# Gated recurrence and squared-relu layers: two pieces of group 0's second layer in three passes, four of group 1's, and other times for weight parts and attention

## The chip, the cores and the metric

The kernel runs on one core of one Trainium2 chip. The metric is the device time of one execution in microseconds (us); lower is better. A core has TensorE (PE; its weight loads are listed apart as PEld), VectorE (DVE), ScalarE (ACT), GpSimd (POOL), and SyncE (SP), whose queue here issues every DMA. Matrix products are written to PSUM[...].

## What is computed

The reference first runs a gated recurrence over 4 batches, 8 heads, 768 steps, head size 48, and then two layers on its output:

```python
for t in range(S):
    state = alpha[:, :, t, :, None] * state + np.einsum('bhd,bhe->bhde', k[:, :, t], v[:, :, t])
    y[:, :, t] = np.einsum('bhd,bhde->bhe', q[:, :, t], state)
...
x = np.ascontiguousarray(attn_out.transpose(0, 2, 1, 3)).reshape(B * S, H * D)
...
h = np.maximum(x @ w_in, 0.0)
return (h * h @ w_out).astype(np.float32)
```

x has 3072 tokens of 384 numbers; w_in is 384 x 2048, w_out 2048 x 384. The result is wanted in fp32 accuracy.

## The kernel before

**Groups and layers.** The tokens form 24 blocks of 128 (one chunk of steps of one batch, all heads) and six groups of four blocks, 512 tokens each. Per group the kernel runs attention for its blocks, then layer in (x @ w_in, 16 tiles of 128 hidden numbers, each 128x512), squared relu, and layer out (four token blocks, each a sum over 16 hidden tiles, each product 128x384). Both weight matrices are cut in NW = 8 pieces of two hidden tiles. The weights arrive as eight-byte numbers and are rebuilt as fp32 during group 0's layer in.

**Two ways to multiply.** A plain product is one fp32 matmul, which the profile shows as two instructions. The other way is three passes in fp32r: each operand is split into a near part (a of x or h, b of the weight; ACT, L596 and L551), a rest l (DVE, L547) and a difference d (DVE, L600 for x and h, L547 for the weight), and the product is a·b + l·l + d·d with l and d scaled. Group 0's layer in is plain (ffn_in, L805), and so is its layer out (ffn_out, L825). Groups 1 to 5 have layer in in three passes (in_x does a·b and l·l, in_y does d·d, L622). In layer out, out_plain, out_x (a·b, l·l) and out_y (d·d) all go through of_tile (L701). AT['k0'] says how many of the last pieces of group 0's layer out go in three passes, AT['k1'] the same for group 1; groups 2 to 5 have all eight in three passes. Where plain and three-pass pieces are mixed, the plain sum of a token block is copied out on ACT (L723), the sum of a·b and l·l is combined with it on DVE (L737), and the sum of d·d is added on DVE (L547) before the store. Hidden tiles that go in three passes are split by split_h and diff_h, AT['ahead'] tiles before their use.

**Weight parts.** prepare() makes the parts of one piece in four steps, AT['wstep'] apart: cast_w (ACT, L551), rest_w (DVE, L547), scale_w (ACT, L565, and a store of l to DRAM, L556), diff_w (DVE, L547, and a store of d, L556). The near parts b stay on the chip. The l and d parts are loaded again for each later group by pump() (L589) from a list of what comes next, as soon as fewer than room[0] buffers are taken (AT['room1'] in group 1, AT['room'] later); used() gives a buffer back after its last product and calls pump(). The parts of w_in are made first: those named by AT['w_first'] in group 0, the others in group 1 every AT['w_in_by']. The parts of w_out follow: AT['o0'] in group 0, AT['o1'] and AT['o2'] in group 1. The pieces that go in three passes first come first in the list. AT['str1'] is when group 1 puts the d parts of its own pieces on the list.

**Attention.** Blocks go in pairs. ln takes log alpha (ACT, L244), cs its running sum along the chunk (a matmul with a triangle of ones), eb and ei its exponentials. For blocks before SPLIT = AT['split'], cs is one fp32 matmul (L265); for the others DVE first splits log alpha into hi and lo (L256, L257), and cs is two fp32r matmuls (L268, L269). turn transposes q and k (L482). ga computes scores (L372) and state sums (L395) of the pair's first block and most of y of the pair before (L352), gb the rest of y and the second block. next_state (L421) multiplies the state by the last row of decays, which comes back by DMA (last<-row, L303). ev_part copies y into x (L515, mostly ACT). split_x and diff_x split x for layer in of the next group.

**What sets the order.** There is no automatic scheduler: weave() goes through the list of units of the current group (matmul steps, each with a cost, about one per 0.66 us of PE) and, ahead of each unit, calls the events that are due. An event's due time is in units since the group's start, and each call puts its instructions on the engines' queues there and then. So AT's numbers move instructions within the queue of every engine. Attention of the next group, splits of x, weight parts and loads are all events:

```python
            while events and events[0][0] <= at:
                _, e, given = events.pop(0)
                e(*given)
            f(*args)
            at += cost
```

AT['g0'] and AT['g1'] are the starts of the pairs of blocks in groups 0 and 1, AT['g'] those in later groups; 'ga' and 'gb' say how long after a pair's start its ga and gb come, in groups 1 to 5; 'g0x', 'g1x' and 'gx' are when the splits of x start; 'h0' and 'h1' where the first splits of h stand among the plain units, 'h1by' how far apart; 'evs0' the distance of the copies of x in group 0. All PSUM tiles come from one pool of eight banks, taken in turn.

Of the kernel before, what the change touches and what calls it, by code (L numbers as in the profile page):

```python
# [15 lines left out]


GB = 4
AT = {'evs': 0.4, 'lead': 4, 'post': 3, 'w_first': (43, 45, 47, 49), 'wstep': 1.6, 'w_in_at': 2, 'w_in_by': 3, 'room1': 23, 'room': 25, 's0': 4, 'ahead': 5, 'late': 2, 'xs': 0.2, 'g0': (-0.5, 19.5, 27.5), 'sc0': (2.35, 2.35, 2.35), 'g1': (0.5, 17.0, 30.5), 'g': (2.2, 15.0), 'g1x': 51, 'gx': 47, 'g0x': 54.5, 'k0': 0, 'h0': 16, 'k1': 5, 'h1': 4, 'h1by': 4, 'evs0': 0.3, 'tp': 'ADMD', 'tp1': 'ADAD', 'split': 12, 'o0': (52,), 'o1': (16, 24), 'o2': (20, 26, 30, 37, 38), 'str1': 25.5, 'ga': 9, 'gb': 12.5}


RUN = {0: 128, 32: 32, 64: 64, 96: 32}
# [3 lines left out]
def kernel(  # L26
# [220 lines left out]

    SPLIT = AT["split"]

# [318 lines left out]
    def diff_w(w, p):  # L568
# [5 lines left out]
        for x in "ld":  # L574
            t = made.pop((x, w, p))
            if w == "i" or p >= NW - AT["k0"] or (x == "l" and p >= NW - AT["k1"]):
                here[x, w, p] = t
        pump()

    def prepare(at, w, p):  # L580
        step = AT["wstep"]
        fs = (cast_w, rest_w, scale_w, diff_w)
        return [(at + i * step, f, (w, p)) for i, f in enumerate(fs)]
# [78 lines left out]
    def splits_of_x(at, g):  # L662
        return [(at + i * AT["xs"], f, (g, i % KM)) for i, f in enumerate((split_x,) * KM + (diff_x,) * KM)]

    def layer_in(g):
        units = []
        for n in range(NJ + 2):
            if n < NJ:
                units.append((1.05, in_x, (n,)))
            if 0 <= n - 2 < NJ:  # L670
                units.append((0.53, in_y, (n - 2,)))
            if 0 <= n - AT["post"] < NJ:
                units.append((0, in_post, (n - AT["post"],)))
            if AT["lead"] <= n < AT["lead"] + AHEAD and (g > 1 or AT["k1"] == NW):
# [355 lines left out]
```

## Time and profile before

| | us |
|---|---|
| median of three runs | 523.61 |
| lowest, highest | 522.91, 525.53 |
| the profiled execution | 524.45 |
| span of that execution in the profile | 522.7 |
| group 0: until its layer in / its layer in / its layer out | 36.0 / 44.8 / 49.2 |
| group 1: layer in / layer out | 41.3 / 47.2 |
| groups 2, 3, 4, 5 | 80.3, 79.2, 75.0, 69.7 |

The granted clock of TensorE was 1.00 throughout. The stages are cut by the first and last products of each kind on PE. In the profile, a row of the timeline gives the start in us, the length, the engine, the line of the kernel, what is written and what is read, shapes, how many instructions; in square brackets stands how long the engine had been idle and for whom. A piece of the chain of waits gives start, length, and what ran. A matmul's end is modelled, and rows of matmuls overlap, so paces are read from starts.

### The profile page before, as it was taken

What the parts mean: (1) busy time and instruction counts of PE and PEld (TensorE: products, weight loads), DVE (VectorE), ACT (ScalarE), POOL (GpSimd) and SP (SyncE); (2) the same over time, 40 slices, a digit from 0 to 9 for tenths busy, and PEclk for the clock granted to TensorE, in tenths of its full rate; (3) what the DMA queues carried; (4) which work ended last, traced back from release to release, by engine and by line L of the source; (5) the groups of instructions that cost most, each with busy time, mean ns of one, the idle gap of its engine ahead of it and who ended that gap; (6) DMA issues with size and microseconds to landing.
All of it is one profiled execution on the core that took longest, in us unless ns stands there. A gap on an engine that the chain in (4) does not pass through costs nothing.

```text
span 522.7 us, 12883 instructions
## 1 busy us (share of the span) xinstructions
PE 514.0 (98%) x5268; PEld 418.0 (80%) x5268; DVE 355.4 (68%) x611; ACT 312.7 (60%) x648; POOL 5.3 (1%) x29
## 2 busy tenths in 40 slices
PE   8989999999999999999999999999999999999997
PEld 5764455665787679978899988899988899988997
DVE  4698989864576789766587466588465477363861
ACT  4658785676888797375863275953275774064620
POOL 4000000000000000000000000000000000000000
PEclk9999999999999999999999999999999999999999
DMA  9899677244586983998975787874673544898201
GB/s 150 204 255 232 207 233 221 47 137 182 164 201 183 249 208 120 285 336 219 226 218 177 235 250 197 213 201 148 231 258 132 167 138 141 260 347 287 84 0 60
DMA packets 140850, 101.95 MB, mean 195 GB/s; under 512 B 111460, under 2 KB 114552, under 8 KB 140792
## 3 DMA queue, kind: packets, MB, share of 16 engines
q1 hardware_dynamic: 140792, 101.14, 67.3%
q8 instruction: 41, 0.67, 0.5%
q14 instruction: 17, 0.14, 0.1%
HBM read 83.79 MB, written 17.33 MB: 193 GB/s over the span
## 4 chain that ended last, share of the span: by engine, by line
PE 93%; DVE 2%; DMA 2%; SPq 1%; issue 1%; ACT 0%; DVEq 0%
PE o L701 33%; PE h L622 32%; PE o L825 8%; PE h L805 7%; PE y L352 4%; PE T L482 2%; PE sckv L372 2%; PE sckv L395 2%; PE cs L265 2%; DMA qk_lent<-in_q_dram 1%; SPq L303 1%; SPq L109 1%; DMA a_in<-in_alpha_dram 1%; DVE x L515 0%; PE cs L268 0%
## 5 line engine op out<-in xcount | busy, mean ns | idle before, releaser
L622 PE MATMUL h<-xa,wb 128*128 128x512 f32 x240 | 69.6, 398 | 0.0
L622 PE MATMUL h<-xd,wd 128*128 128x512 f32 x240 | 68.5, 398 | 0.1
L622 PE MATMUL h<-xl,wl 128*128 128x512 f32 x240 | 67.7, 390 | 0.0
L547 DVE TENSOR_TENSOR hid<-h,hid 128x512 f32<-128x512 f32 x40 | 27.6, 689 | 55.2 <-PE h L622 51.4
L515 ACT COPY x<-y 32x256 f32<-32x256 f32 (+2 forms) x132 | 47.2, 365 | 24.1 <-PE y L352 18.6
L639 ACT ACTIVATE h<-h 128x512 f32<-128x512 f32 x40 | 23.3, 581 | 61.2 <-PE h L622 61.2
L622 PEld LDWEIGHTS h<-xl,wl 128*128 128x128 f32 x240 | 45.0, 188 | 9.8
L622 PEld LDWEIGHTS h<-xd,wd 128*128 128x128 f32 x240 | 44.2, 188 | 10.2 <-issue 0.5
L701 PE MATMUL o<-wd,hd 128*128 128x384 f32 x296 | 52.1, 334 | 0.0
L622 PEld LDWEIGHTS h<-xa,wb 128*128 128x128 f32 x240 | 44.3, 188 | 9.7
L701 PEld LDWEIGHTS o<-wd,hd 128*128 128x128 f32 x296 | 51.4, 188 | 0.0
L701 PE MATMUL o<-wb,ha 128*128 128x384 f32 x152 | 50.9, 335 | 0.0
L701 PE MATMUL o<-wl,hl 128*128 128x384 f32 x152 | 50.9, 335 | 0.0
L701 PE MATMUL o<-wb,hx 128*128 128x384 f32 x144 | 48.7, 338 | 0.0
L701 PE MATMUL o<-wl,hx 128*128 128x384 f32 x144 | 48.1, 334 | 0.0
L805 PE MATMUL h<-x,w_in 128*128 128x512 f32 (+1 forms) x108 | 43.6, 551 | 1.2 <-ACT x L515 1.2
L825 PE MATMUL o<-w_out,hid 128*128 128x384 f32 x128 | 42.8, 490 | 0.0
L637 ACT ACTIVATE hid<-h 128x512 f32<-128x512 f32 x40 | 23.9, 599 | 27.8 <-PE h L622 27.7
L805 PEld LDWEIGHTS h<-x,w_in 128*128 128x128 f32 x108 | 19.9, 190 | 21.1 <-issue 17.2
L825 PEld LDWEIGHTS o<-w_out,hid 128*128 128x128 f32 x128 | 23.9, 190 | 16.0
L547 DVE TENSOR_TENSOR hl<-hid,ha 128x512 fp32r<-128x512 f32 x38 | 26.1, 687 | 7.5 <-ACT ha L596 7.5
L596 ACT ACTIVATE ha<-hid 128x512 fp32r<-128x512 f32 x38 | 23.7, 633 | 11.4 <-PE o L701 6.1
(117 smaller groups left out, 896.1 us busy)
## 6 DMA issues: line engine op xcount, KB each, us to landing
wd<-do SPq DMA_DIRECT2D x37, 384.0 KB, 3.2
wl<-li SPq DMA_DIRECT2D x32, 384.0 KB, 4.8
wd<-di SPq DMA_DIRECT2D x32, 384.0 KB, 4.5
wl<-lo SPq DMA_DIRECT2D x32, 384.0 KB, 4.2
raw<-in_moe_w_in_dram SPq DMA_DIRECT2D x8, 768.0 KB, 6.6
raw<-in_moe_w_out_dram SPq DMA_DIRECT2D x8, 768.0 KB, 6.7
v_in<-in_v_dram SPq DMA_DIRECT2D x24, 192.0 KB, 5.0
out_dram<-osb SPq DMA_DIRECT2D x24, 192.0 KB, 1.9
```

The source lines that it names most:

```text
L265: nc.tensor.matmul(out=out, lhsT=causal, rhs=blk[n].pop("la"), start=True, stop=True)
L352: ins = nc.tensor.matmul(out=ys[e][64 * half : 64 * half + D + G * e, m % 2, p // 2, t], lhsT=lhsT, rhs=rhs, start=(half, e) not in seen, ...
L372: nc.tensor.matmul(out=ps[e][HALF[h], 0, p, :], lhsT=ks[rows, p, HALF[h]], rhs=qs[rows, p, HALF[h]], start=True, stop=True, skip_group_che ...
L515: copy(out=x[kk][to : to + m, t : t + 2], in_=blk[n]["y"][e][r : r + m, :, p // 2],)
L547: nc.vector.tensor_tensor(out=o, in0=x, in1=z, op=op)
L596: nc.scalar.activation(out=a, in_=x, func=AF.Copy, scale=NEAR)
L622: nc.tensor.matmul(out=acc["h", j], lhsT=here[w, "i", p][:, kk, jj * 128 : (jj + 1) * 128], rhs=x_parts[x][:, kk], start=start and kk == 0 ...
L637: nc.scalar.activation(out=hid[j], in_=x, func=AF.Copy, scale=E)
L639: nc.scalar.activation(out=x, in_=x, func=AF.Copy, scale=1.0 + E)
L701: nc.tensor.matmul(out=acc[t][:, 0:DM], lhsT=lhs[:, t * C : (t + 1) * C], rhs=rhs, start=start, stop=stop, skip_group_check=True,)
L805: nc.tensor.matmul(out=ps, lhsT=w[:, kk, c0 : c0 + 128], rhs=xT[g][kk][:, cols], start=(kk == 0), stop=(kk == KM - 1),)
L825: nc.tensor.matmul(out=acc[t][:, 0:DM], lhsT=hid[per * i + j][:, t * C : (t + 1) * C], rhs=w_out[i][:, j, :], start=(i == 0 and j == 0), s ...
```

## The change

Only the dictionary AT at line 19 changes. In words: k0 goes from 0 to 2 and k1 from 5 to 4. Group 0 prepares three pieces of w_in instead of four, and two of w_out (6 and 7) instead of one (3); group 1 prepares five of w_in and six of w_out, in the order 4, 5, 0, 1, 2, 3. Blocks 10 and 11 take cs in fp32r (split 10). The pairs of blocks in group 1 start later, the third of group 0 half a unit later, and ga comes one unit later in groups 1 to 5. The splits of x come one unit earlier in groups 1 to 5 and one later in group 0; hidden tiles are split six tiles ahead instead of five. room1 is 22 instead of 23 and str1 24 instead of 25.5. Group 0's units come to 58.5 instead of 60.

```diff
-AT = {'evs': 0.4, 'lead': 4, 'post': 3, 'w_first': (43, 45, 47, 49), 'wstep': 1.6, 'w_in_at': 2, 'w_in_by': 3, 'room1': 23, 'room': 25, 's0': 4, 'ahead': 5, 'late': 2, 'xs': 0.2, 'g0': (-0.5, 19.5, 27.5), 'sc0': (2.35, 2.35, 2.35), 'g1': (0.5, 17.0, 30.5), 'g': (2.2, 15.0), 'g1x': 51, 'gx': 47, 'g0x': 54.5, 'k0': 0, 'h0': 16, 'k1': 5, 'h1': 4, 'h1by': 4, 'evs0': 0.3, 'tp': 'ADMD', 'tp1': 'ADAD', 'split': 12, 'o0': (52,), 'o1': (16, 24), 'o2': (20, 26, 30, 37, 38), 'str1': 25.5, 'ga': 9, 'gb': 12.5}
+AT = {'evs': 0.4, 'lead': 4, 'post': 3, 'w_first': (46.0, 49.5, 53.0), 'wstep': 1.6, 'w_in_at': 2, 'w_in_by': 3.4, 'room1': 22, 'room': 25, 's0': 4, 'ahead': 6, 'late': 2, 'xs': 0.2, 'g0': (-0.5, 19.5, 28.0), 'sc0': (2.35, 2.35, 2.35), 'g1': (2.5, 19.5, 35.0), 'g': (2.2, 15.0), 'g1x': 50, 'gx': 46, 'g0x': 55.5, 'k0': 2, 'h0': 18, 'k1': 4, 'h1': 4, 'h1by': 2, 'evs0': 0.8, 'tp': 'ADMD', 'tp1': 'ADAD', 'split': 10, 'o0': (40, 47), 'o1': (), 'o2': (23, 26, 29, 35, 42, 36), 'str1': 24, 'ga': 10, 'gb': 12.5}
```

## The prediction

> **What bounds the kernel now.** I read the page's header first, then the chain of waits in order of time, then timelines of the places that the change touches. In the header PE is busy nearly all of the span, DVE two thirds, ACT three fifths:
>
> ```profile
> span 522.7 us, 12883 instructions
> PE 514.0 (98%) x5268; PEld 418.0 (80%) x5268; DVE 355.4 (68%) x611; ACT 312.7 (60%) x648; POOL 5.3 (1%) x29
> PE 93%; DVE 2%; DMA 2%; SPq 1%; issue 1%; ACT 0%; DVEq 0%
> ```
>
> Read in the last line that the chain runs through PE for 93%; the rest lies almost all in the first 36 us (loads and the first blocks). After that the largest idle stretches on PE are a late third-pass weight part at 222.8 us (about 0.3) and an "issue" gap at 261.6 (0.28), so what counts is how long PE's instructions take. The chain gives their pace without the modelled ends (start, length, piece of chain):
>
> ```profile
> 121.23 9.23 PE o L825 x28
> 175.07 5.36 PE o L701 x16
> 269.46 29.32 PE o L701 x168
> 453.19 32.68 PE h L622 x144
> ```
>
> L825 and the x16 of L701 are fp32 products of layer out, two instructions each: 9.23 / 28 x 2 = 0.659 us per product of 128x384. The x168 are products in three passes: 29.32 / 168 x 3 = 0.524. So a product in three passes is 0.136 cheaper. The other price is that of cs, the running sum of logs (first two rows of group 1's layer in, then group 2's):
>
> ```profile
> 162.91 0.81 PE L265 MATMUL cs<-a_in,causal 128*128 128x384 f32 x2
> 163.26 1.16 PE L622 MATMUL h<-xd,wd 128*128 128x512 f32 x3
> 164.25 0.85 PE L622 MATMUL h<-xa,wb 128*128 128x512 f32 x3
> ...
> 248.65 0.34 PE L268 MATMUL cs<-hi,causal_r 128*128 128x384 f32 x1
> ...
> 249.36 0.63 PE L622 MATMUL h<-xa,wb 128*128 128x512 f32 x2
> ```
>
> From the fp32 cs to the second group of L622 pass 1.34 us. Three L622 matmuls of it are 3 x 0.227 (32.68 / 144) = 0.68, so a cs costs 0.66; part of it shows only as a late start of the matmul after it. In two fp32r passes, two blocks take 249.36 - 248.65 = 0.71, or 0.355 each.
>
> **The skill.** "Perfetto Trace Analysis", Identifying the Most-Contended Engine, says that busy matmul time doesn't measure headroom, since matmuls overlap. The trace agrees: the L701 rows are 334 ns long and start 174.5 ns apart; I price by starts. "TensorE: Matmul & The Clock Gate", Back-to-back issue gap, gives N / 2.4 + 2.5 ns for an isolated warm matmul, 162.5 ns at N = 384; the trace has 174.5, and the trace decides. It has no row for fp32. The same page, Architectural detail, calls ACT and DVE strict FIFOs: an instruction that waits holds everything behind it. The trace agrees: in
>
> ```profile
> 242.72 0.36 DVE L421 TENSOR_TENSOR s<-s,last 128x192 f32<-128x192 f32 x1 [3.82 <-DMA last<-row]
> 243.00 0.68 DVE L651 SCALAR_TENSOR_TENSOR hid<-hid 128x512 f32<-128x512 f32 x1
> 243.60 0.68 DVE L547 TENSOR_TENSOR hid<-h,hid 128x512 f32<-128x512 f32 x1
> ```
>
> DVE stands 3.82 us for a DMA, and the eviction of h behind it ends at 244.28, just before PE goes on at about 244.4.
>
> **The change, part by part.**
> (1) k0 0 to 2: in group 0, pieces 6 and 7 of layer out go to three passes: 4 hid tiles x 4 token blocks = 16 products x 0.136 = -2.17 us of PE.
> (2) k1 5 to 4: in group 1, one piece goes back to fp32: 8 x 0.136 = +1.08.
> (3) split 12 to 10: blocks 10 and 11 take the fp32r cs: 2 x (0.66 - 0.355) = -0.61.
> PE's work: -2.17 + 1.08 - 0.61 = -1.70 us. All of it lies on the path, as PE doesn't wait there.
> (4) Added beside PE: group 0 splits four hid tiles, group 1 two fewer, so two more in all: ACT 2 x 0.63 (L596), DVE 2 x (0.69 + 0.69) (L547, L600). Group 0 also gets 4 combinations at L737 (0.55) and 4 at L547 (0.56), and blocks 10 and 11 need hi and lo, 2 x (0.35 + 0.56). About 9 us of DVE over the run; the cover is DVE's 32% of idle time, except at the seam in (5).
> (5) The seam from group 0 to group 1. Before, the splits of x stand here:
>
> ```profile
> 127.06 1.67 ACT L596 ACTIVATE xa<-x 128x512 fp32r<-128x512 f32 x3
> 127.72 1.90 DVE L547 TENSOR_TENSOR xl<-x,xa 128x512 fp32r<-128x512 f32 x3 [3.55 <-ACT xa L596]
> 129.53 1.89 DVE L600 SCALAR_TENSOR_TENSOR xd<-xa,xl 128x512 fp32r<-128x512 f32 x3
> 130.00 1.15 PE L622 MATMUL h<-xa,wb 128*128 128x512 f32 x3
> 130.99 0.39 PE L622 MATMUL h<-xl,wl 128*128 128x512 f32 x1
> ```
>
> The last xl is ready at 129.6, PE needs it at about 131.4: 1.8 us of slack. I walked the new order by laying its instructions end to end at these paces. PE gets there some 2.2 us sooner, while ACT still has the twelve copies of x (L515, 0.37 each, now placed later), a scaling of a weight part (L565, 0.74) and a cast (L551, 0.74) to do between about 121 and 126.6; only then come the three xa. From 126.7, with ACT at 0.55 per xa and DVE at 0.6 per xl, the last xl ends near 129.1 to 129.3, and PE would want it near 128.9. Stall 0.2 to 0.8; I take 0.4. Zero if ACT is a little faster; 1.5 if the weight part's DVE work (0.95 each for rest and diff) holds up xl too. The new L737 of the first token block ends about when PE wants its sum: nothing to 0.3, within that range.
> (6) Weight parts. Group 0 still prepares five pieces (3 of w_in + 2 of w_out, before 4 + 1), group 1 eleven (5 + 6, before 4 + 7). ACT, DVE and the two stores per piece on SP are the same in number and only move past loads and last<-row on SP's queue. The fourth w_in piece now comes in group 1: by my walk its l is cut by 149.1 and wanted at 152.2, the tightest later one has 1.4 us. Cost 0; without the cover, at most 1.4 each.
> (7) Loads. Group 1 has to load the l parts of pieces 6 and 7 again (two more wl<-lo), one wd<-do fewer. With room1 22, the d parts of 6 and 7 are issued late in group 1, at about 207.3 and 208.5, and wanted at about 214.5 and 214.9: 6.4 to 7.2 us. The loads of L589 in the profile took:
>
> ```profile
> DMA to landing us min/median/max: 3.0/3.9/6.0
> ```
>
> So they land in time, by 0.4 at worst as sampled; I take 0.1, between 0 and 4 (a third-pass d part at 222.8 was late already). "DMA: Bandwidth & Descriptors", Latency and other measured facts, has about 2 us of fixed cost per DMA; here even the quickest part takes 3.0.
> (8) ga 9 to 10, ahead 5 to 6, the pairs of group 1 2 to 4.5 units later, gx and g1x a unit earlier, evs0. These move attention, the splits of h and those of x against PE's stream, with no instruction added (ga's empty instruction on POOL goes along; POOL is 1% busy). ga one unit later meets the wait for last<-row later, which shortens it; ahead 6 gives each split one more tile of lead. I count 0, from -0.5 (the small gaps at 222.8 and 261.6 vanish) to +1.5 (a score bank or an eviction comes later than PE wants it, about 0.3 in each of five groups).
>
> Sum: -1.70 + 0.4 + 0.1 = -1.2 us. The profiled execution took 524.45 with a span of 522.7; it would become 523.25 and 521.5. The median shown is 523.61, 0.84 below the profiled run; from it the forecast is 523.61 - 1.2 = 522.4. Half a per cent, 2.6 us, is about what a measurement of this kernel tells from no change (its three runs spread over 522.91 to 525.53).
>
> **Rivals.**
> A. PE's saving arrives whole and the two small gaps go too: -1.70 - 0.3 - 0.3 = -2.3, so 521.3. For it: PE hardly waits today. Against it: the slack at the seam is less than the 2.2 us by which PE comes sooner.
> B. The seam takes it: the stall is 1.5 or more and a second small one follows (the xd splits, 0.6 each, and the first evictions behind the same queue): -1.70 + 2.0, so 523.9. For it: ACT's queue is full for 5 us there. Against it: my walk has the last xl late by 0.8 at most.
> C. Slower: the d parts of pieces 6 and 7 land late at the end of group 1. The load of 7 stands on SP behind the store of a d part of piece 2, which waits for DVE's difference. If it lands in 10 us instead of under 6.4, PE stands 3.6 us; the loads for group 2 behind it (the next one was late by 0.3 already) add perhaps 1.4: -1.70 + 0.4 + 5.0 = +3.7, so 527.3. It decides from a landing of about 6.4 us. For it: DMA is 78% busy in this stage and the wait is for one queue. Against it: no load of this line took over 6.0.
> That the change doesn't do what it says can be left out: the order of instructions shows 16 products more and 8 fewer in three passes, and two fp32 cs fewer.
>
> **Chances.** The forecast, with its own range 521.6 to 523.3, 0.48; A 0.19; B 0.16; C 0.17. Under 521.0 lies most of A (0.15); over 526.2 nearly all of C (0.16); within half a per cent 0.69. The range of 520.7 to 525.9 takes in A with the bound of -0.5 of (8), the forecast, B, and leaves most of C out.
>
> **What would show it.** The chain should show runs of L701 x16 and x32 instead of L825 in group 0, 0.66 per fp32 product and 0.52 in three passes, as before, with 0.7 for the two cs of blocks 10 and 11. PE's first L622 of group 1 should start at about 128, with a wait of 0.2 to 0.8 for xl; without a wait A is right, with over 1.5 B. PE's row L701 wd,hd at about 214 to 215 without a wait for a DMA refutes C. I am wrong if PE's cadence changes where fp32 and fp32r products alternate, or if waits for h or sckv appear in groups 2 to 4, where no product changes.

## The result, and the profile after

The changed kernel takes 523.0 us (median of 20 runs) against 524.77 for the kernel before, run beside it (20 runs): ratio 0.9973, 95% interval 0.9963 to 0.9982. That is 1.4 us less (0.9 to 1.9), where 1.2 were forecast, and inside the half per cent that had the highest chance. The profiled execution has a span of 521.0 us.

The header of the page after, and its chain by engine:

```profile
span 521.0 us, 12919 instructions
PE 511.3 (98%) x5276; PEld 418.5 (80%) x5276; DVE 364.6 (70%) x627; ACT 312.9 (60%) x650; POOL 5.3 (1%) x29
PE 93%; DVE 2%; SPq 2%; DMA 2%; issue 1%; ACT 0%; DVEq 0%
```

PE still carries 93% of the chain. DVE has 9 us more work, as the sum of part (4) had it, and "issue" comes into view. In the chain in order of time (start, length, piece), the pieces at which the stages begin, and one that nobody forecast:

```profile
35.23 9.72 PE h L805 x26
79.76 9.03 PE o L701 x28
120.31 7.41 PE o L701 x40
127.72 6.41 PE h L622 x27
175.70 1.47 PE y L352 x89
202.00 1.41 PE y L352 x88
203.41 1.07 issue
204.48 0.33 PE y L352 x4
217.87 6.17 PE h L622 x27
267.81 29.32 PE o L701 x168
297.13 6.17 PE h L622 x27
```

The paces are those of before: 29.32 / 168 again. At 203.41 PE stands 1.07 us for nothing that the profile shows, in the middle of the y products (L352) of group 1. The run of y around it takes 2.81 us in all, the one at 175.70 takes 1.47: the gap costs 1.3 to 1.4 us, about 0.3 more than the wait that is listed.

The same pieces in the chain of before:

```profile
36.27 9.72 PE h L805 x26
130.46 4.10 PE h L622 x18
218.53 4.12 PE h L622 x18
298.78 6.17 PE h L622 x27
```

Cutting both chains at the first long run of L805 and at the first L622 of each group gives the account:

| stretch | before | after | difference | forecast |
|---|---|---|---|---|
| until the x26 run of L805 | 36.27 | 35.23 | -1.04 | 0 |
| group 0 from there | 94.19 | 92.49 | -1.70 | -2.17 + 0.4 = -1.77 |
| group 1 | 88.07 | 90.15 | +2.08 | +1.08 - 0.61 + 0.1 = +0.57 |
| group 2 | 80.25 | 79.26 | -0.99 | 0 (-0.5 to +1.5 for all of part 8) |
| groups 3 to 5 | 223.92 | 223.87 | -0.05 | 0 |

The first row is no effect of the change: five other kernels with the same first instructions (the moves alone, split 12, k0 0, k1 4 and ga 9 below) start that run at 35.2 to 35.4, among them k1 4, which is the kernel before but for one number. The one profiled execution of before was about 1 us late there. So the sum of the two profiles agrees with the medians partly by luck, and it is the stages that have to be explained: group 0 as forecast, groups 1 and 2 not.

The seam between groups 0 and 1, from ACT's, DVE's and PE's timelines:

```profile
126.23 1.67 ACT L596 ACTIVATE xa<-x 128x512 fp32r<-128x512 f32 x3
126.89 1.90 DVE L547 TENSOR_TENSOR xl<-x,xa 128x512 fp32r<-128x512 f32 x3 [0.91 <-ACT xa L596]
127.56 0.89 PE L622 MATMUL h<-xa,wb 128*128 128x512 f32 x3
128.29 1.05 PE L622 MATMUL h<-xl,wl 128*128 128x512 f32 x3
129.18 0.86 PE L622 MATMUL h<-xa,wb 128*128 128x512 f32 x3
```

PE begins group 1 at 127.6, as forecast (about 128), while the last xl ends at 128.8. The three products with xl take 129.18 - 128.29 = 0.89 instead of 0.68. The page's groups of weight loads show the same wait, and a smaller one at the new L737:

```profile
L622 PEld LDWEIGHTS h<-xl,wl 128*128 128x128 f32 x240 | 45.1, 188 | 10.0 <-DVE xl L547 0.4
L701 PEld LDWEIGHTS o<-wd,hd 128*128 128x128 f32 x304 | 52.8, 188 | 0.3 <-DVE osb L737 0.3
```

The load is late by 0.4, but PE loses less here: the chain's run of L701 x40 is 7.41 - 40 x 0.1745 = 0.43 over its pace and the x27 of L622 0.24 over the 6.17 of other groups. Some 0.2 of the first is the usual cost of coming back from y, so the seam costs about 0.4 to 0.5.

### The profile page after: what moved, and what is told of

The parts are those of the page before. It is cut to its first block, busy times and chain, and to the rows that moved or that the text cites. A ratio compares the mean times of both kernels' runs of the same rounds, so it can differ in the third digit from the quotient of the medians.

```text
span 521.0 us, 12919 instructions
## 1 busy us (share of the span) xinstructions
PE 511.3 (98%) x5276; PEld 418.5 (80%) x5276; DVE 364.6 (70%) x627; ACT 312.9 (60%) x650; POOL 5.3 (1%) x29
## 4 chain that ended last, share of the span: by engine, by line
PE 93%; DVE 2%; SPq 2%; DMA 2%; issue 1%; ACT 0%; DVEq 0%
PE o L701 41%; PE h L622 32%; PE h L805 7%; PE y L352 4%; PE T L482 2%; PE sckv L372 2%; PE sckv L395 2%; PE cs L265 1%; DMA qk_lent<-in_q_dram 1%; SPq L109 1%; SPq L303 1%; DMA a_in<-in_alpha_dram 1%; PE cs L268 0%; PE cs L269 0%; DVE x L515 0%
## 5 line engine op out<-in xcount | busy, mean ns | idle before, releaser
L622 PE MATMUL h<-xa,wb 128*128 128x512 f32 x240 | 68.2, 393 | 0.0
L622 PE MATMUL h<-xd,wd 128*128 128x512 f32 x240 | 68.0, 399 | 0.0
L622 PE MATMUL h<-xl,wl 128*128 128x512 f32 x240 | 67.9, 391 | 0.0
L701 PE MATMUL o<-wb,ha 128*128 128x384 f32 x160 | 54.7, 342 | 0.0
L701 PE MATMUL o<-w_out,hid 128*128 128x384 f32 x160 | 54.0, 491 | 0.0
L701 PE MATMUL o<-wd,hd 128*128 128x384 f32 x304 | 53.8, 335 | 0.0
L701 PE MATMUL o<-wl,hl 128*128 128x384 f32 x160 | 53.6, 335 | 0.0
L622 PEld LDWEIGHTS h<-xl,wl 128*128 128x128 f32 x240 | 45.1, 188 | 10.0 <-DVE xl L547 0.4
L701 PEld LDWEIGHTS o<-wd,hd 128*128 128x128 f32 x304 | 52.8, 188 | 0.3 <-DVE osb L737 0.3
L622 PEld LDWEIGHTS h<-xa,wb 128*128 128x128 f32 x240 | 44.7, 188 | 9.3 <-ACT xa L596 0.2
L622 PEld LDWEIGHTS h<-xd,wd 128*128 128x128 f32 x240 | 44.2, 188 | 9.6
L701 PE MATMUL o<-wb,hx 128*128 128x384 f32 x144 | 48.7, 338 | 0.0
L701 PE MATMUL o<-wl,hx 128*128 128x384 f32 x144 | 48.2, 335 | 0.0
L701 PEld LDWEIGHTS o<-w_out,hid 128*128 128x128 f32 x160 | 29.9, 190 | 19.3
L805 PE MATMUL h<-x,w_in 128*128 128x512 f32 (+1 forms) x108 | 43.6, 552 | 1.2 <-ACT x L515 1.2
L596 ACT ACTIVATE ha<-hid 128x512 fp32r<-128x512 f32 x40 | 25.6, 640 | 25.1 <-DVE hx L547 15.8
L805 PEld LDWEIGHTS h<-x,w_in 128*128 128x128 f32 x108 | 20.0, 190 | 21.0 <-issue 16.9
L547 DVE TENSOR_TENSOR hl<-hid,ha 128x512 fp32r<-128x512 f32 x40 | 27.5, 688 | 10.0 <-ACT ha L596 10.0
```

The source lines that it names most:

```text
L547: nc.vector.tensor_tensor(out=o, in0=x, in1=z, op=op)
L596: nc.scalar.activation(out=a, in_=x, func=AF.Copy, scale=NEAR)
L622: nc.tensor.matmul(out=acc["h", j], lhsT=here[w, "i", p][:, kk, jj * 128 : (jj + 1) * 128], rhs=x_parts[x][:, kk], start=start and kk == 0 ...
L701: nc.tensor.matmul(out=acc[t][:, 0:DM], lhsT=lhs[:, t * C : (t + 1) * C], rhs=rhs, start=start, stop=stop, skip_group_check=True,)
L805: nc.tensor.matmul(out=ps, lhsT=w[:, kk, c0 : c0 + 128], rhs=xT[g][kk][:, cols], start=(kk == 0), stop=(kk == KM - 1),)
```

## The experiments

"Gaps taken off" below means: span, less the start of the x26 run, less the "issue" waits listed for PE. It is 484.7 for the changed kernel (521.0 - 35.23 - 1.1) and 486.1 for the one before (522.7 - 36.27 - 0.3): with one gap each, the change without start and gaps is worth 1.4 us. As a gap costs about 0.3 more than its listed wait, a kernel with more of them comes out too high by about 0.3 for each.

**The moves alone.**

```diff
-'k0': 2, 'k1': 4, 'split': 10
+'k0': 0, 'k1': 5, 'split': 12
```

> The times of the changed kernel with k0 0, k1 5 and split 12 as before: only the moves. If the gain is PE's work alone, this gives it all back (+1.7 us against the changed kernel) and takes away the wait at the seam (-0.4): within 0.5 us of the kernel before, ratio 0.999 to 1.001. If the moves themselves bring about 1 us (the gaps in group 2 that the profile after no longer shows), the ratio is about 0.998.

Measured: 536.0 us, ratio 1.0203 (1.0182 to 1.0223). Both expectations miss by 10 us. PE's waits in this kernel:

```profile
PE T L482 <- DVE k_in L284: 3.3, 1, 3.3
PE T L482 <- DVE q_in L284: 2.8, 2, 2.3
PE o L701 <- issue: 1.4, 1, 1.4
PE y L352 <- issue: 1.2, 1, 1.2
```

Group 1 takes 230.12 - 129.47 = 100.65 us, 10.5 more than in the changed kernel; the chain leaves PE from 184 to 206 and runs through ACT's copies of x and the splits of weights and of ten hidden tiles on DVE, one after the other. With k1 5 and the new times they fall together; k1 4 leaves eight tiles to split. Split 12 alone and k0 0 alone (below) bring nothing of this size, which points to k1 5, though the changed kernel with k1 5 alone was not run. The new times are no gain in themselves.

**Split 12.**

```diff
-'split': 10
+'split': 12
```

> The changed kernel with split 12. By PE's prices the two cs of blocks 10 and 11 cost 0.66 instead of 0.355 each again: +0.6 us against the changed kernel, ratio to before about 0.9985; in the profile two fp32 cs with 1.34 us to the second L622 group after each. If DVE's hi and lo of these blocks held something up, the ratio stays at 0.997 or falls.

Measured: 523.79 us, ratio 0.9975 (0.9962 to 0.9988). The timing can't tell 0.6 us, but the profile can: gaps taken off, 521.6 - 35.17 - 1.2 = 485.2, +0.5 against the changed kernel, and the two fp32 cs are back:

```profile
161.74 0.81 PE L265 MATMUL cs<-a_in,causal 128*128 128x384 f32 x2
162.09 1.15 PE L622 MATMUL h<-xd,wd 128*128 128x512 f32 x3
163.08 0.81 PE L265 MATMUL cs<-a_in,causal 128*128 128x384 f32 x2
```

From one cs to the next 1.34 us, with three L622 in between: the price of 0.66 per cs stands.

**Group 0 in fp32.**

```diff
-'k0': 2
+'k0': 0
```

> The changed kernel with k0 0: group 0's layer out all fp32. Theory of PE's prices: 16 products x 0.136 = +2.2 us, less the wait at the seam of about 0.4, so +1.8 against the changed kernel, ratio to before about 1.0007. Rival, that the seam took more than 0.5: +1.2 or less, ratio under 0.9997.

Measured: 526.93 us, ratio 1.0029 (1.0015 to 1.0043): 3 us over the changed kernel, not 1.8. Group 0 takes 129.58 - 35.39 = 94.19, +1.70 against 92.49, about the 1.8 expected; its first L622 x27 takes 6.14, so the wait at the seam is gone. The rest is "issue" again, now at three places and 3.0 us instead of 1.1:

```profile
PE y L352 <- issue: 1.6, 2, 1.1
PE o L701 <- issue: 1.4, 1, 1.4
```

Gaps taken off it is 486.7, +2.0; with 0.3 more for each of three gaps against one, it is about +1.4, a little under the 1.8 expected.

**One piece fewer in group 1, in the kernel before.**

```diff
-'k1': 5
+'k1': 4
```

> The kernel before with k1 4 alone: one piece of group 1's layer out in fp32. By PE's prices 8 products x 0.136 = +1.1 us in group 1, ratio 1.002, plus or minus what the gaps at the ends of instruction blocks do, as PE's stream is 16 instructions shorter from there (up to 1 us). Rival, that PE waited for parts of the fifth piece: no loss or a gain.

Measured: 525.85 us, ratio 1.0026 (1.001 to 1.0042). Group 1 takes 218.46 - 129.37 = 89.09 against 88.07 before: +1.02, for 1.08 worked out. Group 2 has two gaps of "issue", 1.1 in all, where before had 0.3.

**What the gaps are.** They stood at different places in different kernels. I counted PE's instructions in each trace in order of start (matmuls, weight loads, and semaphore instructions, from 0) up to each gap within a stretch of work. The last instruction ahead of the gap was number 4544 in the changed kernel and with split 12, 6080 in the kernel before, 3776 and 4544 with the moves alone, 3776, 5312 and 6080 with k0 0, 5312 and 6080 with k1 4. All are 192 past a multiple of 256; the waits for DVE stand anywhere. The page lists what brings instructions in:

```profile
q8 instruction: 42, 0.69, 0.5%
```

0.69 MB in 42 packets for 10,704 PE instructions: about 16.4 KB and 256 instructions per packet (the Trainium skill, "Perfetto Trace Analysis", The 4-stage abstract model, has them at 64 bytes each, which agrees). And the 256 instructions ahead of a gap mostly went by in 1.9 to 2.0 us, in the runs of scores, state sums and y (ga), against 521 / 42 = 12 us on average. So I took the gap for PE running out of instructions, and moved the ends of the blocks by putting instructions ahead of everything:

```diff
-    for _ in range(3):
+    for _ in range(2):
         warm(0)
+    ps = ps_att.tile([128, NP, 64], FP32, tag="att", name="small")
+    for _ in range(17):
+        nc.tensor.matmul(
+            out=ps[0:64, 0, :], lhsT=s_t[0][0:D, 0, :], rhs=s_t[0][0:D, 1, :],
+            start=True, stop=True,
+        )
```

> The changed kernel with one warm-up matmul fewer and 17 small ones of zeros at the start, where PE waits for its first inputs: 64 PE instructions more, ahead of everything. Theory: the gap of 1.07 us at 203.4 is PE out of instructions, which arrive in blocks of 256; both gaps seen (203.4 after, 261.3 before) stand 192 instructions past a multiple of 256, each at the end of a block that PE ran through in 1.9 us. With 64 more the block ends elsewhere, no block goes by in under 2.5 us, and the gap is gone: about -1 us against the changed kernel, ratio to before 0.995 to 0.9955. Rival, that the gap is a wait for data at that product: it stays, ratio 0.9973.

Measured: 525.41 us, ratio 1.0013 (1.0004 to 1.0022): slower, where -1 was expected. The products at the start were not free: 34 instructions took 3.82 us, all to one place of PSUM, and the x26 run began at 38.44 instead of 35.23. But the gap at y in group 1 is gone, and one stands at another place and line, again 192 past a multiple of 256 (number 7360):

```profile
322.39 0.96 PE L628 MATMUL h<-xl,wl 128*128 128x512 f32 x3 [0.85 <-issue]
```

A wait for data would have stayed at its product. Gaps taken off it is 484.7, the changed kernel's own number. Then the shift through the filler matmuls of the prologue, by two sizes:

```diff
+    fillers = [7, 7, 7, 7]
...
-        for _ in range(3):
+        for _ in range(fillers.pop(0)):
             nc.tensor.matmul(
-                out=ps[:, 0:NP, :], lhsT=s_t[3].rearrange("a p d -> a (p d)")[:, 0:128],
-                rhs=s_t[3], start=True, stop=True,
+                out=ps[:, 0:2, :], lhsT=s_t[3].rearrange("a p d -> a (p d)")[:, 0:128],
+                rhs=s_t[3][:, 0:2, :], start=True, stop=True,
```

The other size has [12, 12, 11, 11] and 0:1 for 0:2.

> The changed kernel with the 12 filler matmuls of the prologue (4 calls of 3, 256 columns, while PE waits for inputs) as 28 of 128 columns: 64 PE instructions more and no work on the path. Theory of blocks of 256 instructions: the gap of 1.07 at 203.4 is gone; the only gap left is at most the 0.9 seen in group 3 with the same shift. Against the changed kernel -0.2 to -1.1 us, ratio to before 0.995 to 0.997; start of the first L805 run in the chain as before, 35 to 36 us. Rival (a wait for data): gap at the same product of y in group 1.

> The same with 46 fillers of 64 columns: 136 PE instructions more. Here the trace of the changed kernel has five blocks of 256 instructions that PE runs through in under 2.8 us (near 99, 316, 339, 394 and one more), against two. Theory: gaps come at the ends of such blocks, at 192 past a multiple of 256, where transfers are busy: 0 to 3 of them, 0.5 to 1.5 us each, so against the changed kernel -1 to +2.5 us, and none at 203.4. Rival (a wait for data): gap at the same product of y in group 1, and no other.

Measured: 522.86 us, ratio 0.9962 (0.9951 to 0.9974), with one gap of 0.4 in group 3 (number 7360 again), none at 203.4; and 527.3 us, 1.0047 (1.0029 to 1.0066), with three gaps:

```profile
PE y L354 <- issue: 1.0, 1, 1.0
PE o L703 <- issue: 1.0, 1, 1.0
PE h L624 <- issue: 0.5, 1, 0.5
```

They are numbers 2240, 5568 and 8128, all 192 past a multiple of 256, and again none at y of group 1. The x26 run starts at 36.95 and 38.94, as the fillers cost time after all. With starts and gaps taken off the two are at 484.75 and 484.9: between the shifts, little else changed. So the gap at 203.4 belongs to PE's instruction stream and not to data.

That PE waits for the next block of instructions can be read from the traces, which hold the start and length of every q8 packet. Each is 16,384 bytes. Taken in order, packet number k fits the block that begins after number 256 k + 192 (times in us; a stop is counted from one start to the next):

| block end | its packet is over | last start before | next start | after the packet |
|---|---|---|---|---|
| changed kernel, 4544 | 203.04 | 203.19 | 204.48 | 1.44 |
| kernel before, 6080 | 260.13 | 261.07 | 261.56 | 1.43 |
| k0 0, 3776 | 179.23 | 178.65 | 180.66 | 1.43 |
| shift with small products, 7360 | 317.14 | 318.06 | 318.48 | 1.34 |
| changed kernel, 3776 (no stop) | 174.94 | 176.66 | 176.66 | 1.72 |

In the fourteen profiles PE passes 528 such ends after the first 40 us. It stops at 21 of them (19 are listed as "issue", two are too short for that), and each time goes on 1.24 to 1.66 us after the packet was over. At the other 507 the packet had been over for 1.39 us or more when PE came, and it doesn't stop. So a gap appears where PE runs through its block before the next packet has been over for about 1.4 us; near 175 the changed kernel runs through a block as fast, but its packet came in time. What delays a packet in one place and not in another was not looked into.

**ga back to 9.**

```diff
-'ga': 10
+'ga': 9
```

> The changed kernel with ga 9 as before. By part (8) of the prediction the later ga is worth nothing by itself: within 0.4 us of the changed kernel once the gaps at the ends of instruction blocks are taken off, ratio to before 0.996 to 0.999 with them. Rival: the later ga is what removed the loss in group 2 (the profile of before lost about 0.9 us there): +0.5 to +1 us with the gaps taken off, in group 2.

Measured: 524.08 us, ratio 0.9984 (0.9972 to 0.9997). Group 2 takes 297.75 - 218.41 = 79.34 against 79.26, so the later ga isn't what removed the loss there. Gaps taken off (1.2) it is 485.15, +0.45. This kernel has two gaps in group 1, so about 0.3 of it is the second gap's cost beyond its listed wait, and the rest is inside the 0.4 expected.

**The seam earlier.**

```diff
-'w_first': (46.0, 49.5, 53.0), 'evs0': 0.8
+'w_first': (45.0, 48.5, 52.0), 'evs0': 0.4
```

> The changed kernel with the copies of x in group 0 closer together (evs0 0.4) and the three w_in pieces of group 0 prepared one unit earlier: ACT gets to the splits of x sooner. If ACT's queue is what makes PE wait at the seam, the last xl comes about 0.7 us sooner and the wait of about 0.4 to 0.5 us goes: -0.3 to -0.5 against the changed kernel, ratio to before about 0.9965. Rival: DVE's combinations (L737) or the weight parts set it, and it stays: 0.997 or above.

Measured: 524.25 us, ratio 0.9986 (0.9975 to 0.9997): it got worse, by 1.1 with gaps taken off. DVE's and PE's timelines:

```profile
122.21 0.69 DVE L547 TENSOR_TENSOR hl<-hid,ha 128x512 fp32r<-128x512 f32 x1 [1.30 <-ACT ha L596]
122.94 0.69 DVE L600 SCALAR_TENSOR_TENSOR hd<-ha,hl 128x512 fp32r<-128x512 f32 x1
123.55 0.95 DVE L547 TENSOR_TENSOR wd<-wb,wl 128x768 fp32r<-128x768 f32 x1
124.42 0.95 DVE L547 TENSOR_TENSOR wl<-w_in,wb 128x768 fp32r<-128x768 f32 x1
125.29 1.95 DVE L737 SCALAR_TENSOR_TENSOR osb<-o,osb 128x384 f32<-128x384 f32 x4
125.89 3.04 PE L701 MATMUL o<-wd,hd 128*128 128x384 f32 x16 [1.19 <-DVE osb L737]
```

With the weight parts earlier, ACT scales and casts them ahead of the split of the last hidden tile; DVE stands 1.30 for that split, then has two weight parts in its queue ahead of L737, and PE waits 1.19 for L737 before out_y. The three xa begin at 127.34 instead of 126.23, so the earlier xl that was expected did not come about. Two settings moved at once, and whether ACT's copies set the wait for xl stays untested. What the run shows is that at the seam things queue on DVE and ACT, and one that moves up pushes another back.

**A third piece in group 0.**

```diff
-'w_first': (46.0, 49.5, 53.0), 'g0': (-0.5, 19.5, 28.0), 'g0x': 55.5, 'k0': 2, 'h0': 18, 'o0': (40, 47), 'o2': (23, 26, 29, 35, 42, 36)
+'w_first': (45.0, 48.5, 52.0), 'g0': (-0.5, 19.5, 27.2), 'g0x': 54.7, 'k0': 3, 'h0': 14, 'o0': (36.5, 41, 46), 'o2': (26, 29, 35, 42, 36)
```

> The changed kernel with a third piece of group 0's layer out in three passes (k0 3), with its parts prepared in group 0 and the splits and copies placed to suit. By PE's prices 8 products x 0.136 = -1.1 us against the changed kernel, and ratio to before 0.995, if ACT and DVE still cover it. Rival: ACT and DVE are full in that stage (L596, L547, L600 for six hidden tiles and three pieces of weight parts), the wait at the seam grows from about 0.4 to 1.5 or more, and nothing is gained: 0.997 or above.

Measured: 525.16 us, ratio 1.0002 (0.9989 to 1.0015). The rival was right:

```profile
PE o L701 <- DVE osb L737: 2.3, 1, 2.3
```

Here ACT and DVE no longer hide behind layer out of group 0; two pieces are about what they cover as these events are placed.

**The shift without its cost, and with the earlier seam.** In the last filler call one filler instead of three, and 18 small products to different places of PSUM:

```diff
+    more = [0, 0, 0, 18]
...
-        for _ in range(3):
+        for _ in range(1 if more[0] else 3):
...
+        for i in range(more.pop(0)):
+            half = 64 * (i % 2)
+            nc.tensor.matmul(
+                out=ps[half : half + 64, i // 2 % 8, :], lhsT=s_t[3][0:D, 0, :],
+                rhs=s_t[3][0:D, 1, :], start=True, stop=True, skip_group_check=True,
+            )
```

> The shift by 64 PE instructions again, now without a cost in the prologue: two fillers fewer in the last filler call, 18 small products to different places of PSUM instead. As with the first try of this shift, no gap at 203.4, at most 0.6 to 0.9 in group 3, and the first L805 run of the chain at 35 to 36 us instead of 37. Against the changed kernel -0.3 to -1.0 us: ratio to before 0.9955 to 0.9965.

> Both of the last two together, the candidate to beat both kernels: sum of the two, -0.6 to -1.4 us against the changed kernel, ratio to before 0.9948 to 0.9962.

Measured: 522.03 us, ratio 0.994 (0.9922 to 0.9958), and 523.64 us, 0.9977 (0.9961 to 0.9993). The first is faster than both kernels: its interval lies below the changed kernel's 0.9963 to 0.9982 (each taken against the kernel before, in separate sessions). It is a little better than expected. The x26 run starts at 35.32, and group 1 takes 216.56 - 127.77 = 88.79 instead of 90.15: without its gap it is 1.36 shorter. PE's list of waits has no "issue" in it, but group 3 has a stop of 0.4 from start to start at number 7360, too short for that list. The second has the seam's 1.2 at L737 again and a gap of 0.7 at number 7360, so the sum expected of it did not come about.

## Why the prediction was right, point by point

- (1) k0: -2.17 with a wait of 0.4. Group 0 became 1.70 shorter, and undoing k0 alone gave 1.70 back. The mechanism was right, the price 8% too high. The run of 9.23 from which 0.659 was read follows products of y, and coming back from them costs about 0.2; a run x28 that follows cs takes 9.03 (79.76 in the chain after), which gives 9.03 / 28 x 2 = 0.645. From start to start the median is 322 to 323 ns for an fp32 instruction of layer out and 173 in three passes, before and after: 0.126 per product. That makes k0 -2.02, k1 +1.01 and PE's sum -1.62.
- (2) k1: +1.08. Alone in the kernel before, +1.02 in group 1. Right, and nearer still to 1.01.
- (3) split: -0.61. Undone alone, +0.5 once the gaps are off. Right within what one profile tells.
- (4) DVE's 9 us: 364.6 - 355.4 = 9.2. No wait outside the seam shows them, as said. The third piece in group 0 shows how little cover is left: PE waits 2.3 us.
- (5) The seam: 0.4 forecast, about 0.5 found, half in group 0 and 0.24 in group 1's first L622 run, at xl and a little at L737. The size was about right. The order that was walked on ACT is the one in the trace (copies, scaling, cast, then xa); no run shows what the wait would be without it.
- (6) Weight parts at no cost: no wait on them in the profile after. But the moves alone show that the new times cost 11 us, gaps included, where k1 is 5.
- (7) The late d parts: PE's chain has no wait at 212 to 218. The loads of L589 took

```profile
DMA to landing us min/median/max: 3.0/3.9/6.7
```

 The d parts of pieces 6 and 7 were issued at 204.3 and 205.7, about 3 us earlier than worked out. The second landed 6.0 us later, at 211.7, and its products begin at about 215. So rival C did not come, with 3 us to spare instead of 0.4 at worst: the issue times, not the landing, were off.
- (8) Moves at 0, down to -0.5: group 2 lost 0.99. In before it has

```profile
222.78 2.32 PE h L622 x9
260.20 1.09 PE y L352 x67
261.29 0.28 issue
261.56 0.57 PE y L352 x22
```

 The first 27 L622 took 225.10 - 218.53 = 6.57 instead of 6.17, because of the late d part at 222.8, and the run of y 1.94 instead of 1.41. So the two cost 0.40 and 0.53, nearly all of the 0.99. Both are gone, which rival A had as -0.6. The gap of before was the end of an instruction block; the 0.40 also went with k1 4 alone and is absent with ga 9, so it is not the later ga that removed it.
- Missed: the new gap in group 1, which costs 1.36. Its like had been visible before, as the 0.28 at 261.6, which I took for a small fixed loss. Without it, group 1 is 0.72 over before (88.79 - 88.07), for 0.57 forecast: that is +1.08 - 0.61 and the 0.24 of the seam, and nothing for late loads.

So the terms of PE's sum were right one by one, within 8%. The total came out near -1.2 partly by luck: what it left out, -0.99 in group 2 and +1.36 in group 1, largely cancels. How long start and gaps were in the executions that were not profiled isn't known; the 20 runs of before spread over 522.9 to 527.3 us, those of the changed kernel over 522.7 to 524.9. The kernel with the shift and no cost at the start is 0.6% faster than the kernel before, but that compares it with a before whose own gap was not moved away; with gaps and start off both, the change is worth the 1.4 us above, of which 0.40 is the late d part of before.

## What to carry to other kernels

Where one engine is busy all the time, price a change by the start-to-start pace of its instructions, stage by stage, and compare stages of two traces, not only spans: start-up and gaps of 1 us can hide or feign an effect of this size. When every queue is nearly full, an event that is moved up pushes another back, so the times of a plan belong to the amounts that they were made for. And look at the place of a wait that nothing explains: here it stood at a fixed count of instructions.

## What was unexpected of the hardware

PE can stand in the midst of ready work at the end of a block of 256 of its instructions. In the fourteen profiles all 19 "issue" gaps of PE over 0.15 us after the first 40 us (0.3 to 1.4 us) stood at the same count within the block, after blocks that went by in 1.9 to 3.3 us, and PE went on about 1.4 us after the packet with the next block was over. Small fp32 products of 48x64 that all wrote one place of PSUM took 0.11 us per instruction (3.82 / 34); those to different places took about 0.033 (1.2 us for 36). The first stood at 3 us and the second at 23 us of the prologue, so whether the place in PSUM makes the difference isn't shown.
